# Attention scores of two row blocks made in one visit into one five-bank PSUM tile

## The chip, the cores and the metric

The kernel runs on one core of one Trainium2 chip. The metric is device time in microseconds. The core has a matrix engine (TensorE, "PE" in the profile, with its weight loads as "PEld"), VectorE ("DVE"), ScalarE ("ACT"), GpSimd ("POOL") and a queue engine that issues transfers ("SP"). Each engine works through its own list of instructions in order. Where one engine needs what another makes, it waits for a semaphore, which a program library sets when the kernel is built. PSUM is the small memory that TensorE writes its results to. It has eight banks, and a bank holds 512 fp32 numbers in each of 128 partitions.

## The reference

Attention over 8 batches of 8 heads, with 576 rows of 64 numbers per head, is followed by a two-layer MLP with GELU over 4608 tokens:

```python
scores = scale * np.matmul(q, k.transpose(0, 1, 3, 2))
thresh = np.max(scores, axis=-1, keepdims=True) - tau
scores = np.where(scores >= thresh, scores, -1000000000.0)
scores = scores - np.max(scores, axis=-1, keepdims=True)
attn = np.exp(scores)
attn = attn / (np.sum(attn, axis=-1, keepdims=True) + 1e-09)
attn_out = np.matmul(attn, v)
# (8, 8, 576, 64) -> (4608, 512), then
h = x @ w_in                                  # 512 -> 2048
g = 0.5 * h * (1.0 + erf(h * inv_sqrt2))
out = g @ w_out                               # 2048 -> 512
```

All of it is fp32. So each score row needs a maximum, an exponential, a mask (scores within tau of the maximum) and a sum.

## The kernel before

**Work and loops.** Two heads make a pair; there are 32 pairs. A pair's 576 score rows are cut into four blocks of 128 (for each of the two heads) and one last block in which the 64 remaining rows of both heads stand together. Such a block is a slot: slots 0 to 3 have two heads' 128 x 576 scores, slot 4 has one 128 x 576 tile. The main loop (L1060) visits the slots one after the other. The first four pairs (`EARLY`) come in another order and by other helpers, while the weights are still being converted; the other 28, the late pairs, take five visits each.

**A visit.** `scores` (L394) issues four matmuls into two PSUM tiles, one per head, each of two banks with 288 columns in each bank. The two heads lie in partitions 0 to 63 and 64 to 127, so that the array runs both beside each other. `softmax_head` (L406) issues, for each head, the negated maximum on DVE (L415), the threshold on POOL (L416) and the exponential on ACT (L418). `softmax_tail` (L421) issues the mask with the sum, on DVE (L434). `turn_p` (L488) transposes the masked exponentials on DVE in blocks of 32 (L498, L496), and `regroup` (L504) sends them by SP to the places from which `weigh_v` (L522) multiplies them with v, a pair later, in visit 2. `turn_qk` (L375) transposes the next pair's q and k on DVE in visit 2. `divisors` (L466) and `divide` (L556) bring in the sums.

**What fills TensorE.** The MLP of blocks of 256 tokens is spread over the visits by `fill` (L637) according to a written goal: at the end of each visit it issues as many matmuls of `block_steps` (L602; L613 into `hT`, L628 into `o_ps`) as are due. GELUs wait in a list (`late`) until the next visit or until more than `lag` are in it (L573). All this, the transposed tiles of the early pairs and `weigh_v` take one-bank PSUM tiles of the tag `mm`, of which there are four; the scores have the tag `sc`, two tiles of two banks.

**The end stage.** The last ten token blocks are multiplied by a scheme with fewer products (`last_blocks`, L973). `product` (L799, recorded at L801) writes a PSUM bank that `bank` (L804) hands out, and `taken` (L809) reads it at once: DVE adds it (recorded at L683), or ACT copies it (L812). `chain` (L828) orders seven products over two or three banks, so that several other products stand between two uses of a bank.

The order within each engine is that in which the code issues. The library adds the waits.

## Time and profile before

| what | us |
|---|---|
| median of 3 runs (1352.51 to 1354.1) | 1352.98 |
| the profiled execution's own time | 1353.51 |
| span in its profile, first to last instruction | 1351.4 |
| TensorE busy | 1323.0 |
| DVE busy | 1048.1 |
| ACT busy | 605.0 |
| POOL busy | 659.0 |

The busy times are sums over the span, and engines overlap, so that they don't add up. A matmul of the code is two records in the trace. A group of instructions stands under the line of the code that issued it; for the end stage these are the lines of the helpers. Times in the trace count from the first instruction.

### The profile page before, as it was taken

How to read it: one execution, taken by the hardware profiler on the slowest of the kernel's cores; microseconds unless marked ns; L12 is line 12 of the kernel's file. 1: busy time of each engine (PE TensorE's matmuls, PEld its weight loads, DVE VectorE, ACT ScalarE, POOL GpSimd, SP SyncE). 2: the span in 40 equal slices, each digit the busy share in tenths (PEclk: the TensorE clock that was granted, in tenths of full speed). 3: DMA queues.
4: the chain of work that ended last, by engine and by line, in shares of the span. 5: the costliest groups of instructions: out<-in, count | busy, mean ns of one | idle time of the engine just before them, and what ended most of it. 6: DMA issues, size and time to landing. Idle time of an engine off the chain costs nothing.

```text
span 1351.4 us, 19821 instructions
## 1 busy us (share of the span) xinstructions
PE 1323.0 (98%) x6282; PEld 893.8 (66%) x6282; DVE 1048.1 (78%) x1997; ACT 605.0 (45%) x1027; POOL 659.0 (49%) x1097
## 2 busy tenths in 40 slices
PE   8799899999999999999999999999999999999998
PEld 6476557467467557557557557568787787877877
DVE  6987677788888888888888888874758698385765
ACT  7876527548547538537638636413201112211120
POOL 5785354555555554554554551144363513635530
PEclk9899999999999999999999999999999999999999
DMA  8642276677777787687687777500000041000003
GB/s 268 187 151 52 58 164 156 146 162 185 155 180 182 161 193 178 160 207 172 153 208 180 155 179 152 117 9 0 1 0 1 14 112 32 0 1 0 1 0 78
DMA packets 209781, 152.39 MB, mean 113 GB/s; under 512 B 113360, under 2 KB 193088, under 8 KB 209680
## 3 DMA queue, kind: packets, MB, share of 16 engines
q1 hardware_dynamic: 188224, 112.53, 37.5%
q0 software_dynamic: 21024, 38.32, 9.9%
q8 instruction: 51, 0.84, 0.3%
q14 instruction: 50, 0.41, 0.1%
q10 hardware_dynamic: 432, 0.30, 0.1%
HBM read 55.97 MB, written 12.52 MB: 51 GB/s over the span
## 4 chain that ended last, share of the span: by engine, by line
PE 93%; DVE 3%; ACT 3%; DMA 1%; issue 1%; SPq 0%; POOL 0%; DVEq 0%; ACTq 0%; POOLq 0%
PE bank L801 34%; PE o_ps L628 17%; PE hT L613 16%; PE sc L403 14%; PE xT L537 11%; ACT p L418 1%; DMA x<-xall 1%; DVE nmx L415 1%; DVE p L434 1%; PE tr L349 1%; ACT pT L356 1%; DVE power L212 0%; ACT power L202 0%; DVE power L210 0%; PE tr L456 0%
## 5 line engine op out<-in xcount | busy, mean ns | idle before, releaser
L418 ACT ACTIVATE p<-sc,nmx 128x576 f32<-128x576 f32 x288 | 201.9, 738 | 284.0 <-DVE nmx L415 283.7
L434 DVE SCALAR_TENSOR_TENSOR p<-sc,thr,p 128x576 f32<-128x576 f32 x288 | 225.3, 816 | 70.1 <-ACT p L418 68.6
L416 POOL TENSOR_SCALAR thr<-nmx,tau_eff 128x1 f32<-128x1 f32 x288 | 88.0, 307 | 368.0 <-DVE nmx L415 355.8
L415 DVE TENSOR_REDUCE nmx<-sc 128x1 f32<-128x576 f32 x288 | 205.4, 750 | 53.5 <-PE sc L403 52.3
L613 PE MATMUL hT<-xall,w_in 128*128 128x256 f32 x1024 | 241.8, 385 | 0.0
L628 PE MATMUL o_ps<-w_out,g 128*128 128x512 f32 x512 | 236.8, 603 | 0.0
L613 PEld LDWEIGHTS hT<-xall,w_in 128*128 128x128 f32 x1024 | 189.4, 190 | 50.0 <-issue 23.0
L683 DVE TENSOR_TENSOR c<-c,bank 128x320 f32<-128x320 f32 x304 | 147.3, 488 | 33.6 <-PE bank L801 20.1
L683 DVE TENSOR_TENSOR o<-o,bank 128x256 f32<-128x256 f32 x240 | 99.8, 420 | 93.7 <-PE bank L801 88.7
L403 PE MATMUL sc<-kT,qT 64*128 64x288 f32 x960 | 161.8, 431 | 9.3 <-DVE p L434 8.6
L537 PE MATMUL xT<-pT,v 128*64 128x256 f32 (+1 forms) x1280 | 169.3, 418 | 0.8 <-DVE pT L360 0.5
L628 PEld LDWEIGHTS o_ps<-w_out,g 128*128 128x128 f32 x512 | 93.1, 190 | 109.1 <-issue 106.8
L498 DVE STREAM_TRANSPOSE turned_p<-p 128x1152 f32<-128x1152 f32 x112 | 154.4, 1378 | 3.9
L403 PEld LDWEIGHTS sc<-kT,qT 64*128 64x128 f32 x960 | 92.4, 187 | 83.8 <-issue 69.7
L537 PEld LDWEIGHTS xT<-pT,v 128*64 128x64 f32 x1280 | 93.0, 140 | 75.4 <-issue 15.1
L801 PE MATMUL bank<-w_out,c 128*128 128x256 f32 x480 | 120.2, 381 | 0.5 <-DVE o L683 0.5
L269 POOL DMA_DIRECT2D v<-in_v_dram x208 | 110.9, 536 | 3.9 <-issue 1.9
L801 PEld LDWEIGHTS bank<-w_out,c 128*128 128x128 f32 x480 | 89.9, 190 | 18.8 <-DVE o L683 3.0
L854 ACT ACTIVATE c<-c 128x320 f32<-128x320 f32 (+1 forms) x80 | 46.9, 623 | 114.6 <-DVE c L683 114.6
L683 POOL TENSOR_TENSOR c<-c,g 128x320 f32<-128x320 f32 (+1 forms) x40 | 50.5, 1271 | 67.4 <-DVE c L683 67.4
L801 PE MATMUL bank<-t_out,c 128*128 128x256 f32 x320 | 82.7, 381 | 0.0
L801 PE MATMUL bank<-t_out,g 128*128 128x256 f32 x320 | 82.1, 379 | 0.0
(179 smaller groups left out, 1775.1 us busy)
## 6 DMA issues: line engine op xcount, KB each, us to landing
pT<-turned_p SPq DMA_DIRECT2D x448, 160.0 KB, 3.6
pT<-pd_tail SPq DMA_DIRECT2D x112, 80.0 KB, 3.0
q<-in_q_dram POOLq DMA_DIRECT2D x104, 72.0 KB, 3.4
k<-in_k_dram POOLq DMA_DIRECT2D x104, 72.0 KB, 3.2
inv<-turned SPq DMA_DIRECT2D x54, 128.0 KB, 3.9
v<-in_v_dram POOLq DMA_DIRECT2D x156, 40.0 KB, 3.1
out_dram<-o SPq DMA_DIRECT2D x40, 128.0 KB, 2.4
xall<-in_moe_w_out_dram POOLq DMA_DIRECT2D x9, 512.0 KB, 3.8
```

What stands on the lines that cost most here:

```text
L269: eng.dma_start(t[r:P:4, e, 0:n, :], rows[:, r * KR:r * KR + n, :])
L403: nc.tensor.matmul(sc[e][:, h, 0:HALF], lhsT=lhsT, rhs=s["kT"][rows, at:at + HALF], start=True, stop=True)
L415: nc.vector.tensor_reduce(nmx[:, e:e + 1], sc, axis=AXIS.XY, op=ALU.max, negate=True)
L416: nc.gpsimd.tensor_scalar(thr[:, e:e + 1], nmx[:, e:e + 1], -1.0, tau_eff, op0=ALU.mult, op1=ALU.subtract)
L418: nc.scalar.activation(w[:, e * S:(e + 1) * S].rearrange("p (h s) -> p h s", h=2), sc, AF.Exp, bias=nmx[:, e:e + 1], scale=1.0)
L434: nc.vector.scalar_tensor_tensor(row, sc[e][:, :, 0:HALF], thr[:, e:e + 1], row, op0=ALU.is_ge, op1=ALU.mult, accum_out=den[e])
L498: nc.vector.transpose(turned_p[:, :, i // 2, 0:NB, i % 2 * Q:(i % 2 + 1) * Q], w.rearrange("p (e b i) -> p e b i", e=2, i=Q))
L537: nc.tensor.matmul(to, lhsT=s["v"][:, e, c, :], rhs=rhs, start=(c == 0), stop=(c == KR - 1))
L613: nc.tensor.matmul(hT[:, j % 2, :], lhsT=w_in_sb[c][:, j * P:(j + 1) * P], rhs=x_blk[n][:, c, :], start=(c == 0), stop=(c == N_DM - 1))
L628: nc.tensor.matmul(o[:, 0:d_model], lhsT=g[j][:, m * P:(m + 1) * P], rhs=w_out_sb[j], start=(j == 0), stop=(j == N_DF - 1))
L683: eng.tensor_tensor(out, a, b, op=ALU.add)
L801: nc.tensor.matmul(to, lhsT=l, rhs=r, start=start and k == 0, stop=k == len(pairs) - 1, skip_group_check=not start)
```

## The change

The two score tiles become one tile `sc_all` of five banks, in which four score areas of 576 columns are placed by `SC_AT`, two areas for each of two slots. As an area then crosses a bank's end, its two matmuls have unequal widths (512 and 64, 128 and 448, 448 and 128, 64 and 512). In a late pair, visits 0 and 2 issue the scores of two slots, and then the maxima, thresholds and exponentials of both; visits 1 and 3 issue neither. Slot 4 stays alone, and `flip` exchanges the two slots' areas from pair to pair. One piece of 128 columns shares a bank with the other head's area; it is issued first, as a matmul over all 128 partitions, with the new tile `k_end`, whose other half is zero and which ACT fills in each pair.

The `mm` tag has three banks instead of four. Where an early helper took an `mm` tile, it now takes `sc_all`'s last bank each fourth time (`spare_bank`). In the end stage `bank` hands out banks of `sc_all` for all `sc` products and for each second `mm` product. The GELU lag goes from 2 to 1.

```diff
-    ps = ctx.enter_context(tc.tile_pool(name="ps", bufs=4, space=PSUM))
+    ps = ctx.enter_context(tc.tile_pool(name="ps", bufs=3, space=PSUM))
+    BANK = 512
+    sc_all = ps.tile([P, 5 * BANK], FP32, tag="sc", name="sc", bufs=1)
+    SC_AT = {(0, 0): 0, (1, 0): S, (0, 1): 5 * BANK - 2 * S, (1, 1): 5 * BANK - S}
+    flip = [0]
+    CUT = 2 * BANK - S
+    spare = [0]
+    def spare_bank():
+        spare[0] = (spare[0] + 1) % 4
+        if spare[0] or (EARLY in st and ("sc", 1) in st[EARLY]):
+            return ps.tile([P, BANK], FP32, tag="mm", name="tr")
+        return sc_all[:, 4 * BANK:5 * BANK]
...
+    k_end = att.tile([P, 2 * S - 2 * 512], FP32, name="k_end")
...
-            tr = ps.tile([P, NC, P], FP32, tag="mm", name="tr")
+            tr = spare_bank().rearrange("p (c s) -> p c s", s=P)
...
         nc.vector.transpose(kT.rearrange("p (b i) -> p b i", i=Q), ks)
+        nc.scalar.copy(k_end[0:D, :], kT[0:D, CUT:S])
...
     def scores(p, i):
         s = st[p]
-        n = 1 if i == NC else 2
-        sc = s["sc", i] = [ps.tile([P, 2, 512], FP32, tag="sc", name="sc", bufs=2) for _ in range(n)]
-        for h in range(2):
-            for e in range(n):
-                rows = slice(0, P) if i == NC else slice(e * D, (e + 1) * D)
-                lhsT = s["q_tail"] if i == NC else s["qT"][rows, i * P:(i + 1) * P]
-                at = h * HALF + (TAIL if p < EARLY and e == 0 else 0)
-                nc.tensor.matmul(
-                    sc[e][:, h, 0:HALF], lhsT=lhsT, rhs=s["kT"][rows, at:at + HALF], start=True, stop=True)
+        if p >= EARLY and i < NC and i % 2:
+            return
+        first = flip[0] if p >= EARLY else 0
+        todo = [i, i + 1] if p >= EARLY and i < NC else [i]
+        parts = []
+        for k, c in enumerate(todo):
+            pair = (first + k) % 2
+            heads = range(1 if c == NC else 2)
+            s["sc", c] = [sc_all[:, SC_AT[pair, e]:SC_AT[pair, e] + S] for e in heads]
+            for e in heads:
+                cut = -SC_AT[pair, e] % BANK or BANK
+                start = 0
+                for lo, hi in (0, cut), (cut, S):
+                    whole = c < NC and pair == 1 and e == 0 and lo == CUT
+                    parts.append((-1 if whole else k, start, e, c, lo, hi))
+                    start += hi - lo
+        for k, _, e, c, lo, hi in sorted(parts):
+            rows = slice(0, P) if c == NC or k < 0 else slice(e * D, (e + 1) * D)
+            lhsT = s["q_tail"] if c == NC else s["qT"][rows, c * P:(c + 1) * P]
+            at = TAIL if p < EARLY and e == 0 else 0
+            rhs = k_end if k < 0 else s["kT"][rows, at + lo:at + hi]
+            nc.tensor.matmul(s["sc", c][e][:, lo:hi], lhsT=lhsT, rhs=rhs, start=True, stop=True)
+        if i == NC and p >= EARLY:
+            flip[0] ^= 1
...
-            nc.vector.tensor_reduce(nmx[:, e:e + 1], sc, axis=AXIS.XY, op=ALU.max, negate=True)
+            nc.vector.tensor_reduce(nmx[:, e:e + 1], sc, axis=AXIS.X, op=ALU.max, negate=True)
...
+    turn = {"sc": 0, "mm": 0}
     def bank(tag, n):
-        if tag == "sc":
-            return ps.tile([P, 2, 512], FP32, tag="sc", name="bank", bufs=2)[:, 0, 0:n]
-        return ps.tile([P, 512], FP32, tag="mm", name="bank")[:, 0:n]
+        turn[tag] += 1
+        k = turn[tag] % (2 if tag == "sc" else 6)
+        if tag == "mm" and k % 2:
+            return ps.tile([P, BANK], FP32, tag="mm", name="bank")[:, 0:n]
+        k = k if tag == "sc" else 2 + k // 2
+        return sc_all[:, k * BANK:k * BANK + n]
...
             scores(p, i)
-            softmax_head(p, i)
+            if early or i == NC:
+                softmax_head(p, i)
+            elif i % 2 == 0:
+                softmax_head(p, i)
+                softmax_head(p, i + 1)
...
-            lag[0] = 2 if p < NP else 0
+            lag[0] = 1 if p < NP else 0
```

More of the change, by code (lines that the diff above doesn't have):

```diff
@@ L324, in turn_qk_early @@
                 copy(kT[:, TAIL:S], src)
-        tr = ps.tile([P, NC, P], FP32, tag="mm", name="tr")
+        tr = spare_bank().rearrange("p (c s) -> p c s", s=P)
         for j, name in enumerate("qk"):
@@ L351, in turn_p_early @@
         for e in range(n):
-            tr = ps.tile([P, NC, P], FP32, tag="mm", name="tr")
+            tr = spare_bank().rearrange("p (c s) -> p c s", s=P)
             for c in range(NC):
@@ L361, in turn_p_early @@
         tails = s["pT"][0][:, NC, :]
-        tr = ps.tile([P, NC, P], FP32, tag="mm", name="tr")
+        tr = spare_bank().rearrange("p (c s) -> p c s", s=P)
         turn(tr[:, 0, :], MAIN if i < NC else S - P)
@@ L413, in softmax_head @@
         for e in range(n):
-            sc = s["sc", i][e][:, :, 0:HALF]
-            nc.vector.tensor_reduce(nmx[:, e:e + 1], sc, axis=AXIS.XY, op=ALU.max, negate=True)
+            sc = s["sc", i][e]
+            nc.vector.tensor_reduce(nmx[:, e:e + 1], sc, axis=AXIS.X, op=ALU.max, negate=True)
             nc.gpsimd.tensor_scalar(
@@ L418, in softmax_head @@
             nc.scalar.activation(
-                w[:, e * S:(e + 1) * S].rearrange("p (h s) -> p h s", h=2), sc, AF.Exp, bias=nmx[:, e:e + 1], scale=1.0)
+                w[:, e * S:(e + 1) * S], sc, AF.Exp, bias=nmx[:, e:e + 1], scale=1.0)
     def softmax_tail(p, i):
@@ L432, in softmax_tail @@
         for e in range(n):
-            row = w[:, e * S:(e + 1) * S].rearrange("p (h s) -> p h s", h=2)
+            row = w[:, e * S:(e + 1) * S]
             nc.vector.scalar_tensor_tensor(
-                row, sc[e][:, :, 0:HALF], thr[:, e:e + 1], row, op0=ALU.is_ge, op1=ALU.mult, accum_out=den[e])
+                row, sc[e], thr[:, e:e + 1], row, op0=ALU.is_ge, op1=ALU.mult, accum_out=den[e])
         if p < EARLY:
@@ L449, in divide_early @@
         b, hp = divmod(p, HP)
-        tr = ps.tile([P, 512], FP32, tag="mm", name="tr")
+        tr = spare_bank()
         for i in range(lo // P, -(-hi // P)):
@@ L1021 @@
     load_early(2)
-    for t in q_tail + v_sb:
+    for t in q_tail + v_sb + [k_end]:
         nc.gpsimd.memset(t, 0.0)
```

## The prediction

> **What bounds the kernel now.** I read the shares of the page first, then the chain that ended last, the stages, and then single visits in the timeline.

> ```profile
> PE 1323.0 (98%) x6282; PEld 893.8 (66%) x6282; DVE 1048.1 (78%) x1997; ACT 605.0 (45%) x1027; POOL 659.0 (49%) x1097
> ...
> PE bank L801 34%; PE o_ps L628 17%; PE hT L613 16%; PE sc L403 14%; PE xT L537 11%; ACT p L418 1%; DMA x<-xall 1%; DVE nmx L415 1%; DVE p L434 1%; PE tr L349 1%; ACT pT L356 1%; DVE power L212 0%; ACT power L202 0%; DVE power L210 0%; PE tr L456 0%
> ```

> TensorE is the bound, with no slack in the middle. By stage (PE, PEld, DVE, ACT, POOL busy):

> ```profile
> 0.00:145.00 145.00, 124.85 (x831) 90.56 (x833) 110.39 (x217) 108.02 (x219) 93.24 (x154) 0.95 0.52 153
> 145.00:870.00 725.00, 721.62 (x3472) 434.08 (x3469) 609.67 (x1094) 405.40 (x619) 368.82 (x756) 1.00 0.74 167
> 870.00:891.00 21.00, 21.00 (x78) 9.73 (x77) 16.18 (x30) 1.44 (x4) 3.29 (x5) 1.00 0.10 26
> 891.00:1351.00 460.00, 455.52 (x1905) 359.45 (x1903) 311.86 (x658) 90.17 (x186) 193.69 (x183) 1.00 0.07 18
> ```

> Early pairs take 145 us. The 28 late pairs take 725, or 25.9 each, with DVE busy 84% of it: PE leads, DVE follows closely. The end stage (blocks 8 to 17 of the MLP) takes 460. How PE, DVE and ACT overlap in one visit:

> ```profile
> 524.26 1.24 PE L403 MATMUL sc<-kT,qT 64*128 64x288 f32 x8
> ...
> 525.60 1.42 DVE L415 TENSOR_REDUCE nmx<-sc 128x1 f32<-128x576 f32 x2
> 526.39 1.41 ACT L418 ACTIVATE p<-sc,nmx 128x576 f32<-128x576 f32 x2 [0.77 <-DVE nmx L415]
> ...
> 527.24 0.82 DVE L434 SCALAR_TENSOR_TENSOR p<-sc,thr,p 128x576 f32<-128x576 f32 x1 [0.21 <-ACT p L418]
> ...
> 528.83 1.38 DVE L498 STREAM_TRANSPOSE turned_p<-p 128x1152 f32<-128x1152 f32 x1
> ```

> The second maximum runs on DVE while ACT makes the first exponential: two maxima fit in 1.42. From maximum to exponential is 0.79, from exponential to mask 0.85. In the end stage:

> ```profile
> 1010.15 0.70 PE L801 MATMUL bank<-x,s_in 128*128 128x320 f32 x2
> ...
> 1010.69 0.70 PE L801 MATMUL bank<-x,s_out 128*128 128x320 f32 x2
> ...
> 1010.89 0.42 ACT L812 COPY g<-bank 128x320 f32<-128x320 f32 x1
> ```

> A product ends 0.70 after its start, its reader starts 0.04 later, and the next product had already started at 0.54. PE never waits for the reader; the banks are separate tiles.

> [...] after PE's 3.6 us wait before the scores at 48.1 it shows

> ```profile
> 48.00:54.80 6.80, 6.69 (x26) 3.99 (x28) 6.77 (x14) 4.38 (x9) 5.55 (x9) 0.50 0.66 211
> ```

> [...] a score visit (64-row tiles) costs 1.37 us around 0.96 us of streaming.

> **The waits of the built program.** The diff does not say how finely the one tile sc_all is guarded, so I followed each awaited semaphore value to the instruction that reaches it. In the program before, the second maximum waits only for its own matmul. In the changed one, in every late visit: the first maximum waits for the last of the eight score matmuls; maximum 2 waits for exponential 1, maximum 3 for exponential 2, maximum 4 for exponential 3; the first mask waits for exponential 4; the first score matmul of a visit waits for the last mask of the visit before, also where it writes another bank. In the end stage 728 of 952 matmuls write sc_all, and each product there waits for the read of the previous product there. So sc_all is guarded as a whole: one engine at a time.

> **Late pairs.** *Matmuls.* Entry, scores and exit of one visit take 93+1171+104 ns (extra start distances in the trace), two visits 2.74 us. Afterwards one entry and exit fewer, but the 128-column k_end piece alone (2 passes x 107 = 0.21), and uneven pieces. A 288-column matmul is two records 242 ns apart, so a head's 1152 columns take 1.92; the first weights (347 for 242) and the short pieces, which wait for theirs, add an estimated 0.32: 2.24. Sum 0.09+0.10+0.21+2.24+0.11 = 2.75: no gain. Should the heads run in lockstep, 0.3 more. From release to first maximum about 2.9. *Chain.* Four maxima and exponentials in turn: 4 x 0.79 + 3 x 0.79 (exponential start to next maximum) + 0.84 = 6.4 us, where two pairs of visits needed 1.6 each.
> The DVE loop of one pair, in us:
> - slots 0, 1: scores 2.9 with the semaphore, chain 6.4, two masks 1.6, transpose 1.4, two masks 1.6: 13.9
> - slots 2, 3: the same plus the q and k transposes 1.75: 15.65
> - slot 4: scores 1.45, 0.79+0.84+0.83: 3.9 (its transposes, 1.5, lie under the next scores)

> Sum 33.4 against 25.9, or +7.5. PE's other work (fill, xT) lies inside: after slots 2, 3 it has 9.6 us for a gap of 13, after 0, 1 7.4 for 11.3. So PE now stands still about 3.5 to 3.9 us twice per pair. The 3.2 and 3.6 us waits of the early stage both brought half clock, one of 2.2 did, others of 1.4 to 2.2 did not. I take it half the time: the score batch after it doubles (+2.2 and +1.0), so +1.3 per pair (0 to 3.2). 28 x (7.5+1.3) = **+246** (210 to 300).
> Costed at nothing: the k_end copies (28, estimate 0.27 each) on ACT, which has 8.3 us between two chains for 7.5 of GELUs, table loads and q scaling; behind them wait GELU and exponentials, so if the cover is gone up to 8 us in all. The mm pool of 3 banks and the shorter GELU lag: PE waits for GELUs inside its new idle time; without that, 64 hT tiles x 0.6 would be 38 us. Two more table loads: 2.6. On POOL two thresholds per double visit move ahead of four q or k DMA issues, which so start up to 5 us later; they land 3.4 after issue and are first read by a transpose a pair (over 25 us) later, which is their cover; 5 us per pair if not. The thresholds themselves come 0.3 after each maximum, before the exponential ends. SP's order is unchanged.

> **End stage.** Product in sc_all to the next one there: 320 columns 0.70 + 0.04 + read 0.49 (0.42 on ACT) + semaphore 0.065 (mask end to PE in PE's waits) + weight load no longer hidden 0.075 = 1.35. 256 columns, two matmuls: 1.03+0.04+0.41+0.065+0.075 = 1.6. There are 280 and 224 of them: 378+361 = 739, +9 where a product in another bank outlasts the wait. Streaming alone is 453 (measured 455). **+295** (250 to 340). [...] I take full clock[...].

> **Early pairs.** 20 slots at 7.2 us. The first mask comes 1.6 later (max, exp, max, exp), and where a transposed tile sits in sc_all's last bank the mask also waits for PE's transposes and ACT's copy (0.3 to 0.6 plus ACT's queue), about 2.5 more. Part lies under conversions: I take 2.75 a slot, **+55** (20 to 90).

> Sum: 246+295+55 = +596 on the span of 1351.4, or 1947; the profiled execution took 1353.5 and the median is 1353.0, so about 1.6 lies around the span: **1949**.

> **Rivals.**
> *The merged visit pays off* (other side, 4%): the waits inside sc_all end before PE needs them. Place: first score matmul after a mask. Gain: the delays inside late score visits (9.7 us over 112 visits, starts against the usual 1171 ns) and three waits ahead of them (4.9); cost: 28 x 0.11 for slot 4's and the double visits' matmuls. 1353-14.6+3 = 1342. It decides only if the DVE loop stays below PE's 25.9; for that the chain of 6.4 would have to shrink to about 2.7. For it: 84% DVE leaves 4 us per pair. Against: the waits are in the program.
> *Only the end stage pays* (4%): PE's queue and fill hide the attention loop. 1353+295+55 = 1703. Against: fill cannot pass a waiting score matmul in the queue.
> *The clock falls at every wait* (8%): 3.2 per pair, and 60 us of slowed matmuls in the end stage: 1949+28x1.9+60 = 2062.
> The main case holds 84%.

> **How the numbers follow.** Adding the parts' bounds as independent gives about 75 below and 90 above the forecast, which with the clock rival in makes 1865 to 2050. 0.2% is what a measurement of this kernel tells from no change. Faster 0.03, same 0.02 (the first rival's 4% with part of the hiding elsewhere), slower 0.95.

> **What would show it.** In the changed profile: TensorE near 68% busy; ACT's exponentials waiting for maxima and maxima for exponentials, starts about 1.6 us apart; PE waiting for the masks at the scores, and for readers at L833; distance between late pairs near 34.7; the end stage about 755. A period of 26 or back-to-back maxima would prove me wrong.

## The result and the profile after

The changed kernel takes 2043.8 us (median of four runs, 2042.1 to 2047.1) beside 1352.8 for the kernel before on the same chip: 1.511 times the time before, with a 95% interval of 1.508 to 1.513. The forecast was 1949, with a range of 1865 to 2050.

The shares of the page and the chain that ended last, of the changed kernel:

```profile
PE 1558.9 (76%) x6282; PEld 942.7 (46%) x6282; DVE 1056.4 (52%) x1997; ACT 631.6 (31%) x1057; POOL 659.5 (32%) x1098
...
PE sc L833 22%; PE sc L434 11%; DVE nmx L447 8%; ACT p L450 7%; DVE p L466 5%; PE hT L645 5%; PE bank L833 4%; DVE c L715 4%; PE o_ps L660 4%; PE xT L569 4%; DVE o L715 4%; DVE turned_p L530 2%; DMA k<-in_k_dram 2%; SPq L552 1%; ACT L618 1%
```

Before, the chain was TensorE's almost alone. Now maxima (L447), exponentials (L450), masks (L466) and the readers of the end stage (L715) stand in it beside TensorE: engines take turns. By stage (us from the start; PE, PEld, DVE, ACT, POOL busy; then the granted clock):

```profile
0.00:191.70 191.70, 133.39 (x806) 96.80 (x806) 95.54 (x204) 105.81 (x211) 92.71 (x146) 0.85 0.40 116
191.70:1233.20 1041.50, 821.53 (x3468) 506.84 (x3469) 617.30 (x1086) 427.75 (x651) 368.38 (x759) 0.89 0.51 114
1233.20:1266.00 32.80, 32.80 (x108) 15.10 (x107) 25.79 (x52) 5.56 (x9) 5.91 (x10) 1.00 0.42 93
1266.00:2037.00 771.00, 570.94 (x1905) 323.94 (x1903) 317.39 (x656) 92.44 (x186) 192.50 (x183) 1.00 0.04 10
```

The stages are cut here at the starts of four matmuls: the first score matmul of the first late pair, the first one of the last batch of scores, and the end stage's first and last matmul. Cut in the same way, the kernel before has 137.3, 721.1, 32.8 and 455.4. So the early part grew by 54.4, the late pairs by 320.4 and the end stage by 315.6. DVE's work in the late pairs hardly changed (617 us; 610 in the similar window before), but TensorE now runs at a mean clock of 0.89.

The timeline of one late pair, from the scores of slots 0 and 1 to the attention matmuls of visit 2 (start, duration, and in brackets the idle time before with what ended it):

```profile
535.09 2.33 PE L434 MATMUL sc<-kT,qT 64*128 64x448 f32 x14
...
537.47 0.76 DVE L447 TENSOR_REDUCE nmx<-sc 128x1 f32<-128x576 f32 x1 [1.49 <-PE sc L434]
...
538.26 0.74 ACT L450 ACTIVATE p<-sc,nmx 128x576 f32<-128x576 f32 x1 [4.58 <-DVE nmx L447]
...
539.04 0.76 DVE L447 TENSOR_REDUCE nmx<-sc 128x1 f32<-128x576 f32 x1 [0.81 <-ACT p L450]
...
539.83 0.74 ACT L450 ACTIVATE p<-sc,nmx 128x576 f32<-128x576 f32 x1 [0.82 <-DVE nmx L447]
...
543.81 0.82 DVE L466 SCALAR_TENSOR_TENSOR p<-sc,thr,p 128x576 f32<-128x576 f32 x1 [0.88 <-ACT p L450]
...
548.29 0.80 PE L434 MATMUL sc<-k_end,qT 128*128 128x128 f32 x2 [4.22 <-DVE p L466]
549.02 4.43 PE L434 MATMUL sc<-kT,qT 64*128 64x448 f32 x14
553.38 2.92 PE L569 MATMUL xT<-pT,v 128*64 128x320 f32 x20
...
559.75 1.28 ACT L618 ACT_TABLE_LOAD   x1
...
561.05 0.60 ACT L618 ACTIVATE g<-hT 128x512 f32<-128x512 f32 x1
...
561.70 4.71 PE L569 MATMUL xT<-pT,v 128*64 128x256 f32 x20 [5.40 <-ACT g L618]
```

Three things are to be seen. Each maximum waits for the exponential before it and each exponential for its maximum, 1.57 us from one maximum to the next, so that the first mask comes 6.34 us after the first maximum. TensorE waits 4.22 us for the last mask, and then makes at half speed, in 5.09 us (the granted clock is 0.50 from 546.61 to 553.43), the scores that took 2.68 in the visit before. And later it waits 5.40 us with the second part of xT for a bank that a GELU frees; that GELU stands on ACT behind four exponentials and a table load. In the late pairs these waits sum to (us, times, longest):

```profile
PE sc L434 <- DVE p L466: 123.4, 43, 7.3
PE xT L569 <- ACT g L618: 71.6, 13, 9.2
...
DVE nmx L447 <- ACT p L450: 136.0, 168, 0.9
```

The 168 are three in each of the 56 visits. In the end stage of the changed kernel a product no longer starts under the product before it:

```profile
1430.20 1.13 PE L833 MATMUL sc<-t_out,g 128*128 128x256 f32 x4 [0.52 <-DVE o L715]
...
1431.37 0.42 DVE L715 TENSOR_TENSOR o<-o,sc 128x256 f32<-128x256 f32 x1 [1.22 <-PE sc L833]
...
1431.94 1.10 PE L833 MATMUL sc<-t_out,c 128*128 128x256 f32 x4 [0.61 <-DVE o L715]
...
1433.08 0.42 DVE L715 TENSOR_TENSOR o<-o,sc 128x256 f32<-128x256 f32 x1 [1.29 <-PE sc L833]
1433.55 1.13 PE L833 MATMUL sc<-w_out,c 128*128 128x256 f32 x4 [0.51 <-DVE o L715]
```

Product, reader, product, reader: the starts are 1.74 and 1.61 us apart.

### The profile page after: what moved, and what is told of

It is laid out like the page before. It is cut to its first block, busy times and chain, and to the rows that moved or that the text cites. A ratio compares the mean times of both kernels' runs of the same rounds, so it can differ in the third digit from the quotient of the medians.

```text
span 2041.6 us, 19469 instructions
## 1 busy us (share of the span) xinstructions
PE 1558.9 (76%) x6282; PEld 942.7 (46%) x6282; DVE 1056.4 (52%) x1997; ACT 631.6 (31%) x1057; POOL 659.5 (32%) x1098
## 4 chain that ended last, share of the span: by engine, by line
PE 52%; DVE 25%; ACT 12%; issue 4%; DMA 4%; SPq 2%; POOL 0%; DVEq 0%; ACTq 0%; POOLq 0%
PE sc L833 22%; PE sc L434 11%; DVE nmx L447 8%; ACT p L450 7%; DVE p L466 5%; PE hT L645 5%; PE bank L833 4%; DVE c L715 4%; PE o_ps L660 4%; PE xT L569 4%; DVE o L715 4%; DVE turned_p L530 2%; DMA k<-in_k_dram 2%; SPq L552 1%; ACT L618 1%
## 5 line engine op out<-in xcount | busy, mean ns | idle before, releaser
L447 DVE TENSOR_REDUCE nmx<-sc 128x1 f32<-128x576 f32 x288 | 218.2, 758 | 370.1 <-PE sc L434 220.4
L450 ACT ACTIVATE p<-sc,nmx 128x576 f32<-128x576 f32 x288 | 213.5, 741 | 581.6 <-DVE nmx L447 581.6
L466 DVE SCALAR_TENSOR_TENSOR p<-sc,thr,p 128x576 f32<-128x576 f32 x288 | 224.3, 812 | 134.8 <-ACT p L450 72.4
L645 PE MATMUL hT<-xall,w_in 128*128 128x256 f32 x1024 | 249.8, 399 | 22.4 <-ACT g L618 22.2
L569 PE MATMUL xT<-pT,v 128*64 128x256 f32 (+1 forms) x1280 | 206.7, 480 | 71.6 <-ACT g L618 71.6
L569 PEld LDWEIGHTS xT<-pT,v 128*64 128x64 f32 x1280 | 122.4, 164 | 161.2 <-ACT g L618 79.3
L715 DVE TENSOR_TENSOR o<-o,sc 128x256 f32<-128x256 f32 x194 | 81.8, 421 | 213.6 <-PE sc L833 211.3
L434 PE MATMUL sc<-kT,qT 64*128 64x512 f32 (+2 forms) x848 | 179.3, 547 | 13.2 <-DVE p L466 12.2
L715 DVE TENSOR_TENSOR c<-c,sc 128x320 f32<-128x320 f32 x216 | 105.3, 488 | 152.0 <-PE sc L833 152.0
L833 PE MATMUL sc<-w_out,c 128*128 128x256 f32 x384 | 104.4, 394 | 36.0 <-DVE c L715 19.0
L434 PEld LDWEIGHTS sc<-kT,qT 64*128 64x128 f32 x848 | 107.5, 227 | 50.0 <-issue 24.0
L833 PE MATMUL sc<-t_out,g 128*128 128x256 f32 x320 | 90.5, 405 | 42.0 <-DVE o L715 33.5
L715 POOL TENSOR_TENSOR c<-c,g 128x320 f32<-128x320 f32 (+1 forms) x40 | 50.2, 1264 | 172.0 <-DVE c L715 172.0
L833 PEld LDWEIGHTS sc<-w_out,c 128*128 128x128 f32 x384 | 67.7, 189 | 68.6 <-DVE c L715 30.7
L434 PE MATMUL sc<-k_end,qT 128*128 128x128 f32 x112 | 29.7, 352 | 80.0 <-DVE p L466 80.0
```

The lines of the kernel that those rows point to most:

```text
L434: nc.tensor.matmul(s["sc", c][e][:, lo:hi], lhsT=lhsT, rhs=rhs, start=True, stop=True)
L447: nc.vector.tensor_reduce(nmx[:, e:e + 1], sc, axis=AXIS.X, op=ALU.max, negate=True)
L450: nc.scalar.activation(w[:, e * S:(e + 1) * S], sc, AF.Exp, bias=nmx[:, e:e + 1], scale=1.0)
L466: nc.vector.scalar_tensor_tensor(row, sc[e], thr[:, e:e + 1], row, op0=ALU.is_ge, op1=ALU.mult, accum_out=den[e])
L569: nc.tensor.matmul(to, lhsT=s["v"][:, e, c, :], rhs=rhs, start=(c == 0), stop=(c == KR - 1))
L645: nc.tensor.matmul(hT[:, j % 2, :], lhsT=w_in_sb[c][:, j * P:(j + 1) * P], rhs=x_blk[n][:, c, :], start=(c == 0), stop=(c == N_DM - 1))
```

## The experiments

The theory: the tile that holds all scores is guarded as a whole, and its users take turns, in the loop and in the end stage. The rivals were that the order of banks, the merging itself, the smaller pool of moving banks, or the clock carry the cost. All stages are cut as above; times are medians, while the stages are those of the one profiled execution. The 32.8 us between the late pairs and the end stage are the same in every run, to 0.1.

| kernel | time | early | late pairs | end stage |
|---|---|---|---|---|
| before | 1352.8 | 137.3 | 721.1 | 455.4 |
| changed | 2043.8 | 191.7 | 1041.5 | 771.0 |
| changed, end stage on tiles of its own | 1731.7 | 191.9 | 1043.6 | 455.4 |
| before, both heads in one tile | 1514.5 | 154.6 | 866.9 | 455.4 |
| before, three banks and lag 1 | 1393.3 | 146.5 | 751.7 | 455.4 |
| before, lag 1 alone | 1354.5 | 136.4 | 725.7 | 455.5 |
| changed, GELUs first | 1992.6 | 190.6 | 989.8 | 771.0 |
| the same, waits filled with matmuls | 1957.9 | 191.8 | 956.8 | 770.9 |
| changed, no transposes in the score tile | 2019.8 | 163.3 | 1048.9 | 770.9 |
| changed, maxima first | 1984.9 | 188.7 | 984.3 | 771.0 |
| changed, merging undone | 1930.2 | 189.9 | 927.8 | 771.0 |
| the same, mended | 1920.0 | 191.5 | 917.8 | 770.8 |
| the same, GELUs first | 1880.9 | 189.5 | 882.4 | 770.8 |
| changed, four edits together | 1604.7 | 158.4 | 951.7 | 455.4 |

**The end stage on tiles of its own.** The score tile's pool is closed ahead of the end stage, and each bank is then a tile:

```diff
-        return sc_all[:, k * BANK:k * BANK + n]
+        return endp[0].tile([P, BANK], FP32, tag=f"b{k}", name="sc")[:, 0:n]
...
+    sc_end.close()
+    endp.append(ctx.enter_context(tc.tile_pool(name="endp", bufs=1, space=PSUM)))
     last_blocks()
```

> The changed kernel, except that in the end stage each of the eight banks is a tile of its own (the banks, their order and the products are those of the changed kernel; only the tile through which a product is guarded differs). Theory, that the shared score tile makes each product wait for the reader of the product before it: the end stage falls from 771 us back to about 455 (the kernel before), between 445 and 470, and the time from 2044 to about 1729 (1715 to 1745); the late pairs stay at 1042. Rival, that the order of the banks or the number of them costs the time: the end stage stays near 771 and the time near 2044.

It took 1731.7 us, and the end stage 455.4. Its row in the stages, and two products of it:

```profile
1268.20:1724.00 455.80, 455.29 (x1905) 359.44 (x1903) 310.63 (x656) 90.24 (x186) 193.85 (x183) 1.00 0.07 17
```

```profile
1386.62 0.70 PE L836 MATMUL sc<-xall,s_plain 128*128 128x320 f32 x2
...
1387.16 0.70 PE L836 MATMUL sc<-x,s_in 128*128 128x320 f32 x2
```

The products start 0.54 apart again, under the one before. The number of banks and their order are those of the changed kernel, so the whole +315.6 hangs on how the tile is guarded. In this pair of runs, rotation through separate tiles lets the reading of one product overlap the matmuls of the next (455.4), and rotation inside one tile, as it is guarded here, gives no overlap (771.0).

**Both heads in one tile, in the kernel before.** Nothing else of the change is in it:

```diff
-        sc = s["sc", i] = [ps.tile([P, 2, 512], FP32, tag="sc", name="sc", bufs=2) for _ in range(n)]
+        both = scp.tile([P, 2, 2, 512], FP32, tag="sc", name="sc", bufs=1)
+        sc = s["sc", i] = [both[:, e] for e in range(n)]
```

> The kernel before, except that the scores of the two heads of a slot lie in one tile of four banks instead of two tiles of two. Scores are still made one slot at a time, with the matmuls, the lag and the moving banks of the kernel before, and the end stage keeps its own tiles. Theory, that the guard on a whole tile is the cost and the merging of visits isn't: in each late slot maximum 1 waits for exponential 0, and the scores wait for the slot's last mask; each two-head slot then takes about 6.5 us where it took 5.5, and a pair 30.5 where it took 25.9, so some +129 in the late pairs, +20 to +30 in the early ones, and an end stage at 455; time about 1500 (1470 to 1580, the upper end if TensorE falls to half clock in its waits). Rival, that making the scores of two slots in one visit is the cost: about 1353.

It took 1514.5 us (1.119 times the kernel before, 1.116 to 1.123), with +146 in the late pairs and +17 in the early ones. One slot of it in the timeline:

```profile
603.94 0.76 DVE L419 TENSOR_REDUCE nmx<-sc 128x1 f32<-128x576 f32 x1
...
604.73 0.74 ACT L422 ACTIVATE p<-sc,nmx 128x576 f32<-128x576 f32 x1 [0.46 <-DVE nmx L419]
...
605.50 0.76 DVE L419 TENSOR_REDUCE nmx<-sc 128x1 f32<-128x576 f32 x1 [0.81 <-ACT p L422]
...
607.14 0.82 DVE L438 SCALAR_TENSOR_TENSOR p<-sc,thr,p 128x576 f32<-128x576 f32 x1 [0.88 <-ACT p L422]
...
608.85 1.24 PE L407 MATMUL sc<-kT,qT 64*128 64x288 f32 x8 [1.30 <-DVE p L438]
```

The second maximum waits for the first exponential although they read different banks, and the next scores for the last mask. So the guard costs 146 us in the late pairs without any merging, a little under half of the 320.

**Three banks and lag 1, in the kernel before.** This I had costed at nothing.

```diff
-    ps = ctx.enter_context(tc.tile_pool(name="ps", bufs=4, space=PSUM))
+    ps = ctx.enter_context(tc.tile_pool(name="ps", bufs=3, space=PSUM))
...
-            lag[0] = 2 if p < NP else 0
+            lag[0] = 1 if p < NP else 0
```

> The kernel before, except that in the loop the moving banks are three instead of four and the GELUs lag by one pair of tiles instead of two (the end stage keeps four). Theory, that these cost nothing while TensorE has its work in order: time 1353 to 1368, 0 to +15. Rival, that the smaller pool carries a large part of what the change costs: over 1400.

Both expectations missed: 1393.3 us, 1.030 times the kernel before (1.027 to 1.032), or +40. A wait that TensorE does not have at all in the kernel before now occurs twelve times:

```profile
PE xT L539 <- ACT g L588: 20.1, 12, 1.9
```

The lag alone, with four banks, was then run:

> The kernel before, except that the GELUs lag by one pair of tiles instead of two; the four moving banks stay. It tells what of the 40 us of three banks with lag 1 is the lag. Theory, that it is the lost bank (a matmul takes the bank whose GELU is the youngest and still queued): 1353 us, within 8. Rival, that a GELU issued one tile earlier waits on ACT for its matmuls and holds up what stands behind it: 1370 to 1393.

It took 1354.5 us, 1.0012 times the kernel before (1.0004 to 1.0020), and TensorE has no such wait. So 39 of the 40 us hang on the fourth bank, at a lag of 1; three banks with the old lag of 2 were not run.

**GELUs first.** In the changed kernel, ahead of the late maxima:

```diff
             scores(p, i)
+            if not early and n > BATCH:
+                gelus(0)
+                table()
             if early or i == NC:
                 softmax_head(p, i)
```

> The changed kernel, except that in the late visits the GELUs still owed, and the change of ACT's table after them, are issued ahead of the exponentials instead of behind them. Theory, that of the 74 us by which the late pairs passed the forecast a part is the attention matmuls waiting for a bank that a GELU frees, queued on ACT behind four exponentials: the waits of the xT matmuls for a GELU (71.6 us in 13 pairs) go, and the time falls by 30 to 70 us, to about 1975 to 2015. Rival, that the exponentials' delay sets the end of each pair anyway, so that an ACT that starts them one GELU later loses what TensorE gains: the time stays within 15 us of 2044, or rises.

It took 1992.6 us, with nearly all of the gain in the late pairs. TensorE's waits for masks and GELUs there:

```profile
PE sc L434 <- DVE p L466: 181.9, 58, 7.3
PE xT L569 <- ACT g L618: 9.2, 1, 9.2
```

Of the waits for GELUs (71.6 us at xT, 22.2 at hT, 4.0 at o_ps in the changed kernel) 9.2 are left. The waits for masks grew from 123.4 to 181.9, so that a part of the time only moved there; 52 us were won in the late pairs.

**The waits filled.** In the kernel with GELUs first:

```diff
-                fill(owed, tokens)
+                again[0] = 2 if p < NP and i in (1, 3) else 1
+                fill(owed, tokens)
+                again[0] = 1
```

where `again[0]` is how often each MLP matmul is issued.

> The kernel with the GELUs first (1992.6 us), except that in the visits to slots 1 and 3 of a late pair, just ahead of the scores that wait for masks, each MLP matmul is issued twice, so that TensorE works where it waited (3.9 us before the scores of slots 2 and 3, 3.5 us before those of slot 4). The parts of the MLP's sums made there are taken twice, so its output is another; every other instruction is the same. Theory, that the waits are what lets the granted clock fall to half, and that this makes the batch of slots 2 and 3 last 4.35 us instead of 2.6: the clock is near 1 in the late pairs, and the time falls by 28 x 1.7 = 47 us to about 1946 (1935 to 1965), though more matmuls are run. Rival, that the clock is not what sets the pairs' length: the time stays at 1993 or grows by what the second matmuls take.

It took 1957.9 us: 35 less, though 708 more matmul records were run. The two rows of the late pairs, first with GELUs first and then with the waits filled as well; the clock is the third number from the right:

```profile
190.60:1180.40 989.80, 797.10 (x3468) 477.94 (x3468) 615.01 (x1086) 428.47 (x653) 367.88 (x759) 0.91 0.54 120
```

```profile
191.80:1148.60 956.80, 928.70 (x4176) 577.74 (x4177) 616.73 (x1086) 428.35 (x652) 367.94 (x759) 0.99 0.56 125
```

The batch of slots 2 and 3 lasts 2.65 us on average instead of 4.35, so the clock is what made it long. The gain is under the 47 expected, in part because the first late pair took 9 us longer and the next four together 8 us longer with their doubled matmuls. The median pair fell from 35.1 to 32.8.

**No transposes in the score tile.** `spare_bank` always returns an `mm` tile.

> The changed kernel, except that the early transposes never use the last bank of the score tile: all of them share the three moving banks. Theory, that of the early +54 us about 26 are the guard on the heads' one tile (17) and the smaller pool (9), and the rest is the transposes in the shared tile that wait for a whole slot's masks and hold up the next scores: the time falls by 20 to 30 us, to about 2018 (2012 to 2026). Rival, that with three banks for all transposes the waits only move to the pool: within 8 us of 2044, or above.

It took 2019.8 us, and the early part 163.3 instead of 191.7. Its late pairs came out 7.4 us longer than the changed kernel's, which stays unexplained; that execution was 2.5 us above the median. The early +54.4 is thus made up of 17.3 (the heads' one tile), 9.2 (three banks and lag 1) and 28.4 (transposes in the score tile), which sum to 54.9.

**The merging undone.** In the changed kernel the shared tile, the pool and the lag stay:

```diff
-        if p >= EARLY and i < NC and i % 2:
-            return
-        first = flip[0] if p >= EARLY else 0
-        todo = [i, i + 1] if p >= EARLY and i < NC else [i]
+        first = (flip[0] + (i % 2 if i < NC else 0)) % 2 if p >= EARLY else 0
+        todo = [i]
```

and `softmax_head` is called for each slot.

> The changed kernel with the merging alone undone: scores, maxima and exponentials are made one slot at a time again, in the places of the one shared tile; moving banks, lag, the copies of k_end and the end stage stay as changed. Theory, that the costs add up as the parts measured alone say: late pairs of 721 + 146 (one tile for both heads) + 31 (three banks, lag 1) = 898 us against 1042, early part +54 and end stage 771 as in the changed kernel, so 1898 us (1880 to 1920): two slots in one visit cost 144 us over one slot in one visit under the same guard. Rival, that with the guard there one visit for two slots is the better order, since the chip turns from matmuls to maxima half as often: 2044 or more.

It took 1930.2 us. The forecast of 1898 missed by 32. A part was a flaw of the experiment: slot 3 took its last columns from a copy of k_end that belonged to the next pair, and waited for it. In the mended kernel that copy is issued one visit later.

> The kernel with the merging undone, mended: there the scores of slot 3 took their k_end columns from the next pair's copy, which had been made two visits before, and waited for it (20.4 us in 10 waits); here the copy for the next pair is issued after the scores of slot 3. Theory: those waits go, the late pairs fall from 928 to about 905 us (the 898 of the sum of the parts, and what xT still waits), the time from 1930 to 1908 (1898 to 1920). Rival, that the waits were not on the path: 1925 to 1932.

It took 1920.0: 10 of the 20 us of waits were on the path. What xT still waits for GELUs is in the rest, as the third kernel of this row shows:

> The same, with the GELUs still owed issued ahead of the exponentials in the late visits, as was done with the merged kernel, where it took 52 us. Theory, that a slot's two exponentials hold GELUs up less than four do: the waits of xT for a GELU (27.8 us in 13 waits) go, and the time falls by 15 to 28 us, to about 1888 (1878 to 1898). Rival, that the later exponentials take it back: within 8 us of the run beside it.

It took 1880.9, 39 less, more than the 27.8 us of xT's waits and the 3.6 of hT's together; the late pairs are 882.4. With GELUs first in both kernels, merging costs 989.8 - 882.4 = 107 us, or 3.8 a pair, and as changed 1041.5 - 917.8 = 124. Why it costs rather than saves is argued, not shown by a run of its own. In a single visit DVE's transpose (1.38) lies under the next scores; in a merged visit one of two lies between the masks. And the clock (0.98 in these late pairs against 0.91) falls more often in the longer waits. The median pairs give an estimate of the two shares: 35.1 us merged with GELUs first, 32.8 with the waits filled as well, 31.0 here. So some 2.3 us a pair are the clock's, and some 1.8 stay at full clock. Merged visits without the shared guard were not run: four areas of 576 columns in tiles of their own would take all eight banks.

**Maxima first.** Four maxima, then four exponentials:

```diff
                 softmax_head(p, i)
                 softmax_head(p, i + 1)
+                exponentials(p, i)
+                exponentials(p, i + 1)
```

> The changed kernel, except that the four maxima of a visit are issued first and the four exponentials after them, instead of one and one. Theory, that DVE and ACT take turns at the shared tile because they alternate, and each turn costs a handover: of the eight steps seven are handovers in the changed kernel and one here, about 0.5 us for each visit of two slots; 56 visits give 28 us, the time is about 2016 (2008 to 2030). Rival, that the pairs are set by TensorE's waits for GELUs, or that the exponentials, which now all come late, hold up the GELUs as much: within 10 us of 2044, or above.

It took 1984.9 us, 59 less where 28 were expected. In the timeline, one visit's four of each:

```profile
527.83 2.75 DVE L447 TENSOR_REDUCE nmx<-sc 128x1 f32<-128x576 f32 x4 [3.06 <-PE sc L434]
...
530.67 2.63 ACT L459 ACTIVATE p<-sc,nmx 128x576 f32<-128x576 f32 x4 [10.69 <-PE xT L578]
...
533.41 0.82 DVE L475 SCALAR_TENSOR_TENSOR p<-sc,thr,p 128x576 f32<-128x576 f32 x1 [2.83 <-ACT p L459]
```

From the first maximum to the first mask 5.58 us instead of 6.34, so 0.76 a visit and not 0.5; 56 visits give 43. Of the other 16 us, 3 lie in the early part, where the maxima of the two heads come first as well. The rest go with less half clock (238 us of it in the trace instead of 299) and less wait of xT for GELUs (61.6 instead of 71.6); how they divide was not tried.

**Four edits together.**

> The changed kernel with the four edits together: the end stage's banks as tiles of their own (alone -312 us), the GELUs first (-51), the four maxima ahead of the four exponentials (-59), and no early transposes in the score tile (-24). The merging and its shared tile stay in the loop. Theory, that these waits lie in different places, except that the second and third share a part (the time in which TensorE waits for GELUs in about half of the pairs): the sum would be 1598 us, and between 1575 and 1625 is expected; what is left over the kernel before, some 245 us, is the serial chain of the merged visits. Rival, that GELUs first and maxima first shorten one and the same wait, so that only the larger counts: about 1649, or more if the exponentials, pushed back by both, become the end of each chain.

It took 1604.7 us (1.187 times the kernel before, 1.185 to 1.189), 7 from the sum. The end stage is as before (455.4), and the early part is 21 above. The late pairs, 951.7, keep +231: the two edits in the loop gave 90 of their 109. No kernel with the merged visits and their one tile came near the kernel before, and none of these kernels is faster than it.

## Why the prediction was right, point by point

**The waits of the built program** decided it, and they are what the trace shows: maximum after exponential, first mask after the last exponential, scores after the last mask, product after reader. The chain of four was put at 6.4 us and took 6.34; from the scores' release to the first maximum 2.9 was put and 2.80 measured. The score batch of two slots was put at 2.75 and took 2.57 or 2.68 at full clock. A visit before takes 0.41 us beyond the 0.96 of its streaming (four records of one head 0.24 us apart, with those of the other head beside them: all eight records start within 1.26 us). What the 0.41 us are made of is not shown.

**Late pairs: +246 forecast, +320 measured**, outside the 210 to 300 that was put. The chain of turns was right; two terms were too small.
- *DVE's loop*: 13.9, 15.65 and 3.9 us were forecast. With GELUs first and the waits filled, so nearly without GELU waits and half clock, the medians are 13.61, 15.39 and 3.79. The median pair grew from 25.3 to 32.8, or 7.5, as forecast, though both ends are 0.6 lower than the 25.9 (a mean) and 33.4 that were put. In all it is 956.8 - 721.1 = 236 us where 28 x 7.5 = 210 stood, and some 16 of the 236 are the experiment's own in its first five pairs.
- *Clock*: 1.3 a pair, or 36 us in all, was forecast. Its own figures give more: half of 2.2 + 1.0 is 1.6, which would have made the forecast 1957. The batch of slots 2 and 3 lasted 1.4 us too long on average, that of slot 4 0.2, so 1.6 a pair; filling the waits gave 33 us net in the late pairs.
- *Costed at nothing: three moving banks and the lag.* This step failed. "PE waits for GELUs inside its new idle time" isn't so: the bank that xT needs is freed by a GELU that the change itself puts behind four exponentials, and 13 times TensorE waited for it, up to 9.2 us, in pairs whose next scores then had no mask to wait for: it was not inside other idle time. Putting the GELUs first won 52 us here; the same pool cost 40 in the kernel before, with no merged visits beside it. Whether a fourth bank would win the 52 as well was not run. I had named 38 us as the price without that cover, and left it out of the sum.

**End stage: +295 forecast, +316 measured.** The round trip is the mis-sized term: from one product in the score tile to the next it is 1.42 us on average after 320 columns and 1.67 after 256 (medians 1.39 and 1.65), where 1.35 and 1.6 stood. 280 x 1.42 + 224 x 1.67 is 772, against 739 + 9 forecast. Of a product of 256 columns that has waited, 1.14 and 1.17 us pass to its reader's start in the rows above, where 1.07 was put. The 0.075 put for a weight load was my estimate, without a measurement; in the end stage before, a product of 256 columns lasts 1.03 us in its stream and 1.13 after a wait (at 1345.91). The clock stayed at 1.00; that had been assumed, not shown.

**Early pairs: +55 forecast, +54.4 measured**, but its parts were not as put: the heads' turns gave 17 instead of 32, the transposes in the score tile 28 instead of 23, and 9 came from the pool and lag that were costed at nothing. That the sum agrees is luck.

**The range.** The measured time lies 6 us under its upper end: late pairs and end stage missed on the same side. Added as independent, the bounds of the parts give about 67 below and 79 above the forecast, not 75 and 90, so the range was wider than its own working.

**The signs.** TensorE is 76% busy and not 68%, because matmuls at half clock or after a wait count for longer: the k_end piece 0.80 us at a clock of 0.50 and 0.49 at 1.00, a product of 256 columns 1.13 after a wait and 1.03 without (its busy time rose from 1323 to 1559). The pairs are 37.3 us apart and not 34.7, by the two terms above. The end stage is 771, not 755. The waits named are all there.

**The rivals.** That the merged visit pays off is refuted by the runs with the merging undone: it costs 107 to 124 us. That only the end stage pays is refuted by the late pairs alone. That the clock falls at every wait is nearest in time (2062), but for another reason: the end stage kept full clock, and of 28 batches of slots 2 and 3 eight were made at full speed.

## What to carry to other kernels

A PSUM tile was a unit of waiting here (the end stage took 771.0 us with the five banks in one tile, and 455.4 with each bank as a tile): before several banks are put into one tile, or scratch is borrowed from one, ask who uses its other parts at that time, since one shared tile made 316 us in a stage that has no scores and no merged visits. When stages are merged under such a guard, add up the chain of turns, not the instructions. And where a change takes a bank from a pool, name for each user of the pool the instruction that frees its bank and what stands ahead of that instruction in its queue.

## What the runs showed of the hardware that was not expected

The granted clock did not follow the length of one wait. In the changed kernel TensorE waited 2.08 and 2.44 us before slots 2 and 3 of two pairs (at 363.74 and 254.25), and the batch took 2.68 us, at full speed. In two other pairs it waited only 1.50 and 1.92 us (at 772.47 and 1065.88), and the batch took 5.09 and 5.08. There another wait, of 2.01 and 1.58 us for a GELU, stood just ahead, with 1.12 and 0.70 us of matmuls between the two.

```profile
768.48:771.89 3.41, 1.12 (x2) 0.30 (x2) 3.38 (x8) 3.35 (x5) 1.69 (x3) 1.00 0.49 118
771.89:775.30 3.41, 2.83 (x9) 2.29 (x11) 1.91 (x3) 3.37 (x5) 0.00 (x0) 0.50 0.34 57
...
362.29:365.70 3.41, 1.96 (x14) 1.54 (x16) 2.77 (x5) 0.00 (x0) 0.00 (x0) 1.00 0.68 151
```

The first was 33% busy and half clock followed. The other was 58% busy, and full clock went on. With the whole trace cut so, the 53 stretches at full clock with half clock after them were at most 49% busy with matmuls; those with full clock after them were at least 41% busy. The 54 at half clock that full clock followed were at least 86% busy, and the 33 that half clock followed at most 93%. The end stage kept full clock between its waits, and its emptiest stretch was 51% busy. In the trace of the kernel before, one of 56% had half clock after it. Half clock also outlasted a wait: the one for the masks ended at 548.29, and the clock was 0.50 until 553.43.

Back to back, four maxima take 2.75 us (0.69 each) and four exponentials 2.63 (0.66 each), while a single one takes 0.76 and 0.74, or 0.07 to 0.08 more. Alternating between engines thus cost twice here, by the handover and by this: without it a visit took 0.76 us less from the first maximum to the first mask, 5.58 instead of 6.34.
